# One-core attention and two gated layers: q and k of two runs kept whole, run 0 loaded by head pairs, x in two tiles

## The chip, the cores and the metric

The kernel runs on one core of a Trainium2 chip. The metric is the device time in microseconds (us); lower is better. A profiled execution also leaves a trace, and the trace counts from the first to the last instruction, which it calls the span.

## What is computed

The reference is sliding-window attention with a distance bias, then two gated layers on its output:

```python
scores = scale * np.matmul(q, k.transpose(0, 1, 3, 2))        # 4 batches, 8 heads, 576 positions, 64 wide
mask = (rel >= 0) & (rel < 128)
scores = np.where(mask, scores + bias[None], -1000000000.0)
attn = softmax(scores)                                        # over the keys, float32
x = np.matmul(attn, v)                                        # to 2304 tokens x 512
x = ((x @ w_a) * (x @ w_b)) @ w_out                           # 512 -> 1536 -> 512, weights float64
out = (((x @ w1) * (x @ w2)) @ w3) @ w_out2                   # 512 -> 1024 -> 1024 -> 512
```

q, k, v and the output are float32; the weights come as float64. A product of full precision is made of three TensorE terms of the type fp32r: each operand is split into a rounded `hi` and a rest `lo`, and lo*hi, hi*lo and hi*hi are summed.

## The kernel before

**Attention.** A batch has five blocks of 128 positions (the last has 64), handled in three runs: `RUNS = ((0, 1), (2, 3), (4,))`. A run has four steps, one for each pair of heads, so there are 48 steps in all; steps 0 to 3 are run 0 of batch 0, steps 4 to 7 are run 1, steps 8 to 11 are run 2. A step is: `scores` (TensorE, line 318), `step_exps` (VectorE adds the bias and takes the largest, lines 343 to 348; ScalarE exponentiates, L351), `norms` (VectorE divides by the sum, lines 358 to 365), `probs` (TensorE transposes, L383, then a copy to `pt`), `pv` (TensorE, L404, three steps later: `LAG = 3`) and `pv_out` (ScalarE writes `x_hi`, VectorE writes `x_lo`, lines 418 and 419).

**q and k.** `load_item` brings 128 positions of all heads (256 KB) by one DMA of the SP queue. `prep` transposes them (L282) into PSUM; ScalarE rounds them to `q_th` or `k_th` (L291) and VectorE subtracts the rest into `q_tl` or `k_tl` (L292; the profile shows every such subtraction at line 73, where the helper `sub` is). `scores` then sums the three terms.

**Weights.** `Stages` loads a weight (512 KB), and converts it from float64 in stages: ScalarE makes `ca` (L108) and `ce` (L111), VectorE runs L115, L118, L122 and L127, ScalarE rounds to `wh` (L136), VectorE subtracts to `wl` (line 73). Group 0 has six such weights; two stages' turns are taken in each step of batch 0. A load waits for one of `raws=2` buffers.

**The filler.** Once the six weights of group 0 are whole, `Filler` puts pieces of the first gated layer (`g1`, L546, and `g2_some`, L574) between the steps. The first piece stands behind `pv` of step 4.

**What sets the order.** In the attention part TensorE's order is the program's (`manual_schedule`). The orders of VectorE, ScalarE, GpSimd and SP come from a scheduler that works at build time; each engine then runs its list strictly in order.

**Warm-ups.** `keep_warm` runs matmuls on a constant tile. Ten of 256 columns stand at the start, and `pv` adds one of 512 columns for each full block in batch 0:

```python
            if b == 0 and rn < WARM_RUNS and m == P:
                keep_warm(WARM, warm)
```

**Memory.** `x_hi` and `x_lo` hold all 2304 tokens from the start. The pools `conv_a` and `early_p` (six loads) are closed when group 0's weights are whole, and `acc0` and `acc1` take their place.

Of the kernel before, what the change touches and what calls it, by code (L numbers as in the profile page):

```python
# [29 lines left out]

GROUPS = (6, 4)
TA, TN = 256, 512
LEAD, EARLY, RING = 512, 6, 5
CUTS = (0, 1280, 1792, 2304)
RUNS = ((0, 1), (2, 3), (4,))
LAG = 3
# [1 line left out]
FILL = 1.6  # L38
PACE = (2.0, 1.0)
TURN = 400  # L40
WARM_RUNS, WARM = 3, 1


@with_exitstack
def attention_moe_moe(ctx, tc, q, k, v, w_a, w_b, w_o, w_1, w_2, w_3, w_o2, out):
# [16 lines left out]
    ps_g = ctx.enter_context(tc.tile_pool(name="ps_g", bufs=2, space=PSUM))  # L62

    ident = const.tile([P, P], F32, name="ident")
    x_hi = xp.tile([P, KC, NT], F32R, name="x_hi")
    x_lo = xp.tile([P, KC, NT], F32R, name="x_lo")
    w34 = dram.tile([2, DFF2, DM], F32, name="w34")

    def f32(ap):
# [2 lines left out]
    def sub(eng, out, a, b):  # L72
        eng.tensor_tensor(out=out, in0=a, in1=b, op=ALU.subtract)  # L73
# [177 lines left out]

    def load_item(run, n):
        b, (x, i) = blocks_of(run)[0], items(run)[n]
        if len(items(0)) * run + n < EARLY:
            t = early_p.tile([P, H * D], F32, name="early")
# [16 lines left out]
    def prep(run, n):  # L272
        b, (x, i) = blocks_of(run)[0], items(run)[n]
        m = rows(i)
        hold = []

        def trans():
            ps = ps_t.tile([P, W], F32, name="tr")[:, 0:NP * m].rearrange("p (h c) -> p h c", h=NP)
            hold.append(ps)
            t = raws.pop((b, x, i))  # L280
            for hp in range(NP):
                nc.tensor.transpose(ps[:, hp, :], t[0:m, hp * P:(hp + 1) * P], ident[0:m, 0:m])  # L282

        def parted():
            ps = hold[0]
            if x == 0 and m == LAST:
                dst = [(slice(j * D, (j + 1) * D), q_t2, slice(j * D, (j + 1) * D)) for j in range(2)]
            else:
                dst = [(slice(0, P), k_t if x else q_t, slice(i * P, i * P + m))]
            for o, (hi, lo), c in dst:  # L290
                nc.scalar.activation(hi[o, :, c], ps[o], ACTF.Copy)  # L291
                sub(nc.vector, lo[o, :, c], ps[o], f32(hi[o, :, c]))  # L292

        return trans, parted

# [9 lines left out]
    def scores(st):  # L305
        b, rn, hp = st
        run = RUNS[rn]
        wide = [window(i)[3] == 2 for i in run]
        ps = [ps_s.tile([P, W], F32, name="s") for j in range(2 if any(wide) else 1)]
        at = 0  # L310
        for i in run:
            m, n, nb, nj = window(i)
            ks = slice(max(i - 1, 0) * P, max(i - 1, 0) * P + n)
            for x, (a, c) in enumerate(((1, 0), (0, 1), (0, 0))):
                for j in range(nj):
                    r = slice(j * D, (j + 1) * D) if nj == 2 else slice(0, P)
                    qs = q_t[a][r, hp, i * P:(i + 1) * P] if nj == 2 else q_t2[a][:, hp, :]
                    nc.tensor.matmul(  # L318
                        ps[j][:, at:at + n], qs, k_t[c][r, hp, ks], start=(x == 0), stop=(x == 2)
                    )  # L320
            live[st, i] = dict(ps=[p[:, at:at + n] for p in ps[:nj]])
            at += n
        assert at <= W
# [63 lines left out]
    ready = [0]  # L387
    outs = {}

    def pv(step):  # L390


        b, rn, hp = step
        ps = outs[step] = ps_t.tile([P, W], F32, name="tr")
        at = 0
        for i in RUNS[rn]:
            m, n, nb, nj = window(i)
            t = live.pop((step, i))["pt"]
            for g in range(nb):
# [12 lines left out]
    def pv_out(step):  # L412
        b, rn, hp = step
        run = RUNS[rn]
        m = sum(window(i)[0] for i in run)
        o = slice(b * S + run[0] * P, b * S + run[0] * P + m)
        ps = outs.pop(step)[:, :m]
        nc.scalar.activation(x_hi[:, hp, o], ps, ACTF.Copy)
        sub(nc.vector, x_lo[:, hp, o], ps, f32(x_hi[:, hp, o]))
        if hp == NP - 1:  # L420
            ready[0] = o.stop

# [102 lines left out]
    def g1(g, n, t, tn, zs=range(2), ps=None):  # L525
# [11 lines left out]
        for z in zs:  # L537

            if g:
                ps.append(mm_tile(tn))  # L540
            elif ps[z] is None:
                ps[z] = mm_tile(tn)
            p = ps[z]
            terms = [(w, x, kk) for w, x in ((lo, x_hi), (hi, x_lo), (hi, x_hi)) for kk in range(KC)]
            for y, (w, x, kk) in enumerate(terms):
                nc.tensor.matmul(  # L546
                    p, w[:, z, kk, :], x[:, kk, o], start=(y == 0), stop=(y == len(terms) - 1)
                )
        if zs[-1] == 0:
            return  # L550
# [41 lines left out]
    def g2_feat(g, t, m, tn):  # L592
# [8 lines left out]
        ya = acc[h].rearrange("p (m t) -> p m t", m=KC)[:, m, t0:t0 + tn]  # L601
        nc.vector.tensor_tensor(out=ya, in0=ya, in1=p, op=ALU.add)  # L602
        if g == G1 - 1:
            nc.scalar.activation(x_hi[:, m, o], ya, ACTF.Copy)
            sub(nc.gpsimd, x_lo[:, m, o], ya, f32(x_hi[:, m, o]))

    def g2_tok(g, t, s, tn):
        p = mm_tile(DM)
# [66 lines left out]
    def attention_ops():  # L675

        late = []
        for n in range(NS + LAG):
# [24 lines left out]
    class Filler:  # L703
# [5 lines left out]
        def run(self, owed):  # L709
            self.owed += owed  # L710
            while self.owed > 0 and self.items:
# [2 lines left out]
                    break  # L714
                self.items.pop(0)
                self.owed -= cost
                f()
            self.owed = min(self.owed, 1.0)

# [5 lines left out]
    pools["A", 0] = ctx.enter_context(tc.tile_pool(name="wA0", bufs=1))  # L725
    pools["A", 1] = ctx.enter_context(tc.tile_pool(name="wA1", bufs=1))
    first = ExitStack()
    pools.update(conv=first.enter_context(tc.tile_pool(name="conv_a", bufs=1)), raws=2, cas=3)
    early_p = first.enter_context(tc.tile_pool(name="early_p", bufs=EARLY))
    pools["gate"] = gate_pa  # L730
    pools.update(abufs=1, gbufs=2)

    consts()
    for x in range(len(items(0))):
        load_item(0, x)
    for x in range(len(RUNS[0])):
        load_v(0, x)
    for x in range(len(items(1))):
        load_item(1, x)
        f, g = prep(0, x)  # L740
        f()
        g()
    side.parts += weight_parts(0)
    fl = Filler()
    nc.vector.memset(warm, 0.0)
# [66 lines left out]
```

## Time and profile before

| | |
|---|---|
| runs | median 963.18 us (962.84 to 963.54, 3 runs) |
| profiled execution | 965.76 us, its span 964.0 us, mean granted TensorE clock 0.986 |
| TensorE matmul (PE) | 944.0 us busy, 98% |
| weight load (PEld) | 787.4 us, 82% |
| VectorE (DVE) | 552.1 us, 57% |
| ScalarE (ACT) | 420.6 us, 44% |
| GpSimd (POOL) | 156.9 us, 16% |
| chain that ended last | PE 91%, DVE 5%, ACT 2%, DMA 1% |

Busy shares are means over 964 us. The first 50 us differ from the rest, so the rows below are read by stretch. A matmul in float32 leaves two records in the trace, one in fp32r leaves one. "Granted clock" is a share of full speed: 1.00 is 2.4 GHz, 0.50 is 1.2 GHz.

### The profile page before, as it was taken

To read this page: it belongs to the slowest core of one execution; us is meant where nothing else is said; L and a number is where in the kernel's file an instruction comes from. 1 tells how busy PE (TensorE), PEld (TensorE's weight loads), DVE (VectorE), ACT (ScalarE), POOL (GpSimd) and SP (SyncE) were. 2 spreads that over 40 slices of the span, in tenths; PEclk is the share of its full clock that TensorE was granted. 3 is DMA by queue.
4 is the path that set the end of the run, shared out by engine and by line. 5 is a ranking of instruction groups with operands and counts; after the bars stand their busy time and mean duration, and the time that the engine had idled before them with its cause. 6 is when DMAs were issued, how large, how long until landed. Compare 5 with 4: busy or idle time off the path is not lost.

```text
span 964.0 us, 13974 instructions
## 1 busy us (share of the span) xinstructions
PE 944.0 (98%) x5330; PEld 787.4 (82%) x5330; DVE 552.1 (57%) x1312; ACT 420.6 (44%) x939; POOL 156.9 (16%) x139
## 2 busy tenths in 40 slices
PE   7899999999999999999999999999999999999998
PEld 5588788787888888888888888888888888888886
DVE  6968786854998355866745653822832822521322
ACT  5867777855654344444533531533421421211111
POOL 3000010001112110211110121344212111111111
PEclk8799999999999999999999999999999999999999
DMA  9523333002443222332312320300300300000112
GB/s 213 154 57 71 83 77 68 18 2 88 132 137 103 77 88 91 106 99 78 130 46 97 109 88 1 111 21 0 110 22 1 109 22 1 23 1 0 44 56 99
DMA packets 90371, 68.28 MB, mean 71 GB/s; under 512 B 58304, under 2 KB 79296, under 8 KB 90304
## 3 DMA queue, kind: packets, MB, share of 16 engines
q1 hardware_dynamic: 90304, 67.38, 24.1%
q8 instruction: 42, 0.69, 0.3%
q14 instruction: 25, 0.20, 0.1%
HBM read 58.20 MB, written 8.91 MB: 70 GB/s over the span
## 4 chain that ended last, share of the span: by engine, by line
PE 91%; DVE 5%; ACT 2%; DMA 1%; issue 0%; SPq 0%; POOL 0%; DVEq 0%
PE mm L546 51%; PE mm L598 13%; PE mm L613 10%; PE mm L454 5%; PE tr L404 3%; PE s L318 2%; PE tr L383 2%; PE mm L574 2%; PE tr L282 1%; DVE pe L345 1%; DVE pe L365 1%; ACT pe L351 1%; PE mm L446 1%; PE mm L586 1%; DMA early<-in_k 1%
## 5 line engine op out<-in xcount | busy, mean ns | idle before, releaser
L73 POOL TENSOR_TENSOR gl<-g,gh 128x512 fp32r<-128x512 f32 (+1 forms) x102 | 124.4, 1219 | 790.3 <-ACT gh L558 790.3
L555 DVE TENSOR_TENSOR g<-a,mm 128x512 f32<-128x512 f32 (+1 forms) x102 | 63.4, 622 | 203.1 <-PE mm L546 198.3
L558 ACT ACTIVATE gh<-g 128x512 fp32r<-128x512 f32 (+1 forms) x102 | 59.1, 579 | 152.9 <-DVE g L555 152.4
L553 ACT ACTIVATE a<-mm 128x512 f32<-128x512 f32 (+1 forms) x102 | 55.2, 541 | 126.2 <-PE mm L546 126.2
L546 PE MATMUL mm<-x_hi,wlA 128*128 128x512 f32 (+1 forms) x416 | 102.9, 368 | 0.0
L546 PE MATMUL mm<-x_lo,whA 128*128 128x512 f32 (+1 forms) x416 | 99.6, 361 | 0.0
L546 PE MATMUL mm<-x_hi,whA 128*128 128x512 f32 (+1 forms) x416 | 99.4, 361 | 0.0
L546 PE MATMUL mm<-x_hi,wlB 128*128 128x512 f32 (+1 forms) x400 | 98.9, 369 | 0.1
L546 PE MATMUL mm<-x_lo,whB 128*128 128x512 f32 (+1 forms) x400 | 98.6, 368 | 0.0
L546 PE MATMUL mm<-x_hi,whB 128*128 128x512 f32 (+1 forms) x400 | 98.2, 368 | 0.0
L111 ACT ACTIVATE ce<-raw,pad 128x512 int32<-128x512 uint32 x76 | 57.9, 762 | 65.9 <-DVE ca L127 33.8
L546 PEld LDWEIGHTS mm<-x_lo,whA 128*128 128x128 f32 x416 | 72.5, 189 | 12.2
L546 PEld LDWEIGHTS mm<-x_hi,whA 128*128 128x128 f32 x416 | 72.5, 189 | 12.0
L546 PEld LDWEIGHTS mm<-x_hi,wlB 128*128 128x128 f32 x400 | 71.1, 188 | 13.1 <-ACT acc L590 0.5
L546 PEld LDWEIGHTS mm<-x_lo,whB 128*128 128x128 f32 x400 | 71.1, 189 | 12.5
L546 PEld LDWEIGHTS mm<-x_hi,whB 128*128 128x128 f32 x400 | 71.0, 189 | 12.5
L602 DVE TENSOR_TENSOR acc<-acc,mm 128x512 f32<-128x512 f32 (+1 forms) x100 | 62.2, 629 | 33.1 <-PE mm L598 32.9
L546 PEld LDWEIGHTS mm<-x_hi,wlA 128*128 128x128 f32 x416 | 71.3, 189 | 11.6 <-issue 0.3
L108 ACT ACTIVATE ca<-raw 128x512 f32<-128x512 f32 x76 | 50.6, 666 | 51.0 <-DMA raw<-in_moe_w 23.2
L351 ACT ACTIVATE pe<-pe,st 128x256 f32<-128x256 f32 (+1 forms) x144 | 68.4, 478 | 9.7 <-DVE st L345 9.3
L127 DVE SCALAR_TENSOR_TENSOR ca<-ce,ca 128x512 int32<-128x512 int32 x76 | 58.9, 775 | 13.1 <-ACT ce L111 11.6
L122 DVE SCALAR_TENSOR_TENSOR ca<-raw,ca 128x512 int32<-128x512 int32 x76 | 58.8, 775 | 1.7
(121 smaller groups left out, 1579.2 us busy)
## 6 DMA issues: line engine op xcount, KB each, us to landing
raw<-in_moe_w SPq DMA_DIRECT2D x32, 512.0 KB, 3.6
raw<-in_moe_w_out SPq DMA_DIRECT2D x20, 512.0 KB, 3.5
raw<-in_moe_w_a SPq DMA_DIRECT2D x12, 512.0 KB, 3.6
raw<-in_moe_w_b SPq DMA_DIRECT2D x12, 512.0 KB, 3.5
out<-acc SPq DMA_DIRECT2D x18, 256.0 KB, 2.0
v<-in_v SPq DMA_DIRECT2D x16, 256.0 KB, 4.1
w<-ce SPq DMA_DIRECT2D x16, 256.0 KB, 2.0
raw<-w SPq DMA_DIRECT2D x16, 256.0 KB, 2.9
```

What stands on the lines that cost most here:

```text
L73: eng.tensor_tensor(out=out, in0=a, in1=b, op=ALU.subtract)
L111: nc.scalar.activation(e, lw, ACTF.Relu, bias=seven, scale=-(2.0 ** -29))
L122: nc.vector.scalar_tensor_tensor(out=ai, in0=hw, scalar=-(1 << 30), in1=ai, op0=ALU.bitwise_and, op1=ALU.bitwise_or)
L127: nc.vector.scalar_tensor_tensor(out=ai, in0=es[0], scalar=7, in1=ai, op0=ALU.bitwise_xor, op1=ALU.bitwise_or)
L351: nc.scalar.activation(pe[:, j, :n], pe[:, j, :n], ACTF.Exp, bias=st[:, 0, j:j + 1], scale=-1.0, accum_out=st[:, 1, j:j + 1],)
L546: nc.tensor.matmul(p, w[:, z, kk, :], x[:, kk, o], start=(y == 0), stop=(y == len(terms) - 1))
L553: nc.scalar.activation(a, ps[0], ACTF.Copy)
L555: nc.vector.tensor_tensor(out=gg, in0=a, in1=ps[1], op=ALU.mult)
L558: nc.scalar.activation(gh, gg, ACTF.Copy)
L598: nc.tensor.matmul(p, w, x, start=(y == 0), stop=(y == len(terms) - 1))
L602: nc.vector.tensor_tensor(out=ya, in0=ya, in1=p, op=ALU.add)
L613: nc.tensor.matmul(p, x, w, start=(y == 0), stop=(y == len(terms) - 1))
```

## The change

Five edits go together. (1) `x` is two pairs of tiles: tokens 0 to 1279 from the start, the rest only once the first pools are closed. `pv_out` cuts a step that straddles token 1280 in two. (2) For runs 0 and 1, q and k go unsplit to `w_t` (float32), and their scores are one float32 term in place of three; only k of block 3 is also split, because run 2 needs it. (3) Run 0's q and k come by head pairs: sixteen loads of 64 KB, four for each pair, each pair transposed ahead of its step (`prep_first`). (4) Weights have four load buffers in place of two, and all four loads of run 1 have buffers of their own. (5) The warm-ups in `pv` end with the first filler piece.

```diff
-LEAD, EARLY, RING = 512, 6, 5
+LEAD, EARLY, RING = 512, 4, 5
+WHOLE = 2
...
-WARM_RUNS, WARM = 3, 1
...
-    x_hi = xp.tile([P, KC, NT], F32R, name="x_hi")
-    x_lo = xp.tile([P, KC, NT], F32R, name="x_lo")
+    HALF = CUTS[1]
+    x_t = [[xp.tile([P, KC, HALF], F32R, name=f"x_{z}") for z in ("hi", "lo")]]
...
+    def load_first(hp, x):
+        t = raws[x, hp] = early_p.tile([P, 2, P], F32, name=f"first{x}{hp}")
+        for i in range(2):
+            nc.sync.dma_start(
+                out=t[:, i].rearrange("p (h d) -> p h d", h=2),
+                in_=(q, k)[x][0, 2 * hp:2 * hp + 2, i * P:(i + 1) * P, :].rearrange("h p d -> p h d"),
+            )
...
+            if run < WHOLE:
+                nc.scalar.activation(w_t[x][:, :, i * P:(i + 1) * P], ps, ACTF.Copy)
+                if x == 0 or i < blocks_of(WHOLE - 1)[1][-1]:
+                    return
...
+    def prep_first(hp):
...
+            for x in range(2):
+                raw = raws.pop((x, hp))
+                for i in range(2):
+                    nc.tensor.transpose(ps[:, x, i], raw[:, i], ident)
...
+            for x in range(2):
+                ps = hold[0][:, x].rearrange("p i c -> p (i c)")
+                nc.scalar.activation(w_t[x][:, hp, 0:2 * P], ps, ACTF.Copy)
...
-            for x, (a, c) in enumerate(((1, 0), (0, 1), (0, 0))):
+            one = b == 0 and rn < WHOLE
+            terms = ((0, 0),) if one else ((1, 0), (0, 1), (0, 0))
+            for x, (a, c) in enumerate(terms):
+                qh, kh = (w_t[0], w_t[1]) if one else (q_t[a], k_t[c])
...
-            if b == 0 and rn < WARM_RUNS and m == P:
-                keep_warm(WARM, warm)
+            if not began[0] and m == P:
+                keep_warm(1, warm)
...
+        cut = [o.start] + [HALF] * (o.start < HALF < o.stop) + [o.stop]
+        for a, e in zip(cut, cut[1:]):
+            hi, lo = [t[:, hp] for t in xs(slice(a, e))]
...
+            if run == 0 and hp + 1 < NP:
+                ops += prep_first(hp + 1)
...
-    pools.update(conv=first.enter_context(tc.tile_pool(name="conv_a", bufs=1)), raws=2, cas=3)
-    early_p = first.enter_context(tc.tile_pool(name="early_p", bufs=EARLY))
+    pools.update(conv=first.enter_context(tc.tile_pool(name="conv_a", bufs=1)), raws=4, cas=3)
+    whole_p = first.enter_context(tc.tile_pool(name="whole_p", bufs=1))
+    w_t = [whole_p.tile([P, NP, WHOLE * 2 * P], F32, name=f"w_{x}") for x in "qk"]
+    early_p = first.enter_context(tc.tile_pool(name="early_p", bufs=1))
...
-    for x in range(len(items(0))):
-        load_item(0, x)
-    for x in range(len(RUNS[0])):
-        load_v(0, x)
+    for hp in range(NP):
+        for x in range(2):
+            load_first(hp, x)
+        if hp in (1, 2):
+            load_v(0, hp - 1)
...
+            late_x = ctx.enter_context(tc.tile_pool(name="xp1", bufs=1))
+            x_t.append([late_x.tile([P, KC, NT - HALF], F32R, name=f"x1_{z}") for z in ("hi", "lo")])
```

The lines of the changed kernel stand some 5 to 40 further down: its scores are at L356, bias and largest at L383, ScalarE's exponentials at L389, the division at L403, the weight conversion at L113, L116, L120, L123, L127, L132 and L141, `sub` at L78.

TensorE's start, from the first transposes of q and k (`early` and `first` are loads of them, `tr` and `s` are PSUM tiles) to the scores of step 2. Before:

```order
L282 MATMUL tr<-ident,early 128x128 x16
L318 MATMUL s<-k_th,q_tl 128x128 x2
L318 MATMUL s<-k_tl,q_th 128x128 x2
L318 MATMUL s<-k_th,q_th 128x128 x2
L318 MATMUL s<-k_th,q_tl 128x256 x2
L318 MATMUL s<-k_tl,q_th 128x256 x2
L318 MATMUL s<-k_th,q_th 128x256 x2
L282 MATMUL tr<-ident,early 128x128 x4
```

And now (the ten warm-ups, which stood ahead of it all, are the rows left out):

```order
L322 MATMUL tr<-ident,first_148 128x128 x2
...
L322 MATMUL tr<-ident,first_151 128x128 x2
L356 MATMUL s<-w_k,w_q 128x128 x2
L356 MATMUL s<-w_k,w_q 128x256 x2
L322 MATMUL tr<-ident,first_154 128x128 x2
L322 MATMUL tr<-ident,first_157 128x128 x2
L295 MATMUL tr<-ident,early_176 128x128 x4
L356 MATMUL s<-w_k,w_q 128x128 x2
```

Step 0 needs one head pair in place of all four; the transposes of block 2's q (`early_176`) still stand ahead of the scores of step 1.

ScalarE around the first weight conversion (`ca` and `ce` are the converted weight's tiles, `pt` the transposed probabilities). Before:

```order
L351 ACTIVATE pe,st<-pe,st 128x128
L291 ACTIVATE k_th<-tr 128x4x128
L351 ACTIVATE pe,st<-pe,st 128x256
L268 ACTIVATE pt<-tr 128x512
L291 ACTIVATE q_th<-tr 128x4x128
L108 ACTIVATE ca<-raw 128x512
L111 ACTIVATE ce<-raw,pad 128x512
L351 ACTIVATE pe,st<-pe,st 128x128
```

And now, from the copies of head pair 2 (first two rows) to those of head pair 3 (last two):

```order
L327 ACTIVATE w_q<-tr 128x256
L327 ACTIVATE w_k<-tr 128x256
L304 ACTIVATE w_k<-tr 128x4x128
L281 ACTIVATE pt<-tr 128x512
L389 ACTIVATE pe,st<-pe,st 128x128
L113 ACTIVATE ca<-raw 128x512
L116 ACTIVATE ce<-raw,pad 128x512
L389 ACTIVATE pe,st<-pe,st 128x256
L389 ACTIVATE pe,st<-pe,st 128x128
L327 ACTIVATE w_q<-tr 128x256
L327 ACTIVATE w_k<-tr 128x256
```

The conversion of the first weight has moved into step 2's exponentials, ahead of the copies that step 3's scores need.

VectorE between the bias rows of step 4 and those of step 5. Before, all of it but the first four rows:

```order
L73 TENSOR_TENSOR wlA_240<-ca,whA_239 128x512
L73 TENSOR_TENSOR x_lo<-tr,x_hi 128x256
L358 TENSOR_SCALAR st<-st 128x4
L270 COPY pt<-tr 128x256
L73 TENSOR_TENSOR q_lastl<-tr,q_lasth 64x4x64
L359 RECIPROCAL st<-st 128x4
L115 TENSOR_SCALAR ca<-ca 128x512
L365 TENSOR_SCALAR pe<-pe,st 128x256 x4
L118 TENSOR_SCALAR ca<-ca 128x512
```

And now, its last eleven rows; ten more of the kind stand ahead of them:

```order
L127 SCALAR_TENSOR_TENSOR ca<-raw,ca 128x512
L78 TENSOR_TENSOR wlA_239<-ca,whA_238 128x512
L120 TENSOR_SCALAR ca<-ca 128x512
L283 COPY pt<-tr 128x256
L397 RECIPROCAL st<-st 128x4
L78 TENSOR_TENSOR q_lastl<-tr,q_lasth 64x4x64
L132 SCALAR_TENSOR_TENSOR ca<-ce,ca 128x512
L123 TENSOR_SCALAR ca<-ca 128x512
L120 TENSOR_SCALAR ca<-ca 128x512
L403 TENSOR_SCALAR pe<-pe,st 128x256 x4
L127 SCALAR_TENSOR_TENSOR ca<-raw,ca 128x512
```

More conversions of weights stand between two steps of the attention than before. From step 4's bias to step 5's division VectorE's list now has 17 rows of conversions, where it had 11: one more each of L123 and L127, two more each of L132 and of the subtraction to `wl`; it has one subtraction to `x_lo` less, and two short rows (128x4) more.

## Rows read from the trace of the kernel before

**Rows 1.** Windows, core 0: stretch, length, busy of each engine (instructions), granted clock, DMA share, GB/s.

```profile
11.00:30.00 19.00, 16.67 (x110) 11.90 (x110) 16.94 (x70) 14.76 (x46) 0.00 (x0) 0.73 1.18 234
30.00:45.00 15.00, 10.79 (x80) 6.58 (x79) 14.94 (x59) 13.61 (x40) 0.00 (x0) 0.81 0.52 155
45.00:50.00 5.00, 5.00 (x36) 3.59 (x34) 4.64 (x16) 3.85 (x8) 0.00 (x0) 0.54 0.03 10
50.00:81.00 31.00, 31.00 (x291) 27.41 (x288) 19.87 (x75) 19.60 (x60) 2.19 (x3) 1.00 0.24 54
...
130.00:165.00 35.00, 35.00 (x331) 29.29 (x330) 27.67 (x119) 28.65 (x90) 2.01 (x2) 1.00 0.29 65
```

**Rows 2.** Waits of PE, whole span: waited for, us in total, times, longest.

```profile
PE tr L383 <- DVE pe L365: 9.0, 8, 2.2
...
PE mm L574 <- POOL gl L73: 0.4, 1, 0.4
```

**Rows 3.** Chain of waits, 0 to 110 us: start, length, what; the start.

```profile
2.79 5.10 DMA early<-in_k
...
10.98 0.29 DVE pe L345
...
11.32 1.87 ACT pe L351 x8
```

**Rows 4.** The same chain, VectorE's pace.

```profile
23.66 0.60 DVE ca L122
...
24.67 0.60 DVE ca L127
...
32.08 0.60 DVE wlA L73
...
35.19 0.34 DVE ca L118
...
38.76 0.33 DVE x_lo L73
```

**Rows 5.** The same chain, from step 5's probabilities on.

```profile
44.41 1.94 PE tr L383 x8
46.35 1.58 PE s L318 x9
47.93 1.05 PE tr L404 x8
...
50.48 4.31 PE mm L546 x36
54.79 0.87 PE tr L383 x8
...
56.02 0.59 PE tr L404 x8
56.60 0.32 PE mm L373
...
102.60 0.95 PE s L318 x12
```

**Rows 6.** Timeline of PE: the start's warm-ups, and block 2's q.

```profile
2.83 2.31 PE L373 MATMUL mm<-warm 128*128 128x256 f16 x10 [2.83 <-DVE warm L745]
...
11.64 0.72 PE L282 MATMUL tr<-ident,early 128*128 128x128 f32 x4 [0.81 <-DMA early<-in_q]
```

**Rows 7.** The first weight: issue on SP, from issue to landing, first use on ACT.

```profile
13.70 0.61 SPq L83 DMA_DIRECT2D raw<-in_moe_w_a  x1
...
DMA to landing us min/median/max: 4.9/4.9/4.9
...
18.68 0.67 ACT L108 ACTIVATE ca<-raw 128x512 f32<-128x512 f32 x1
```

**Rows 8.** Timeline of DVE: step 4's first bias row, step 5's division.

```profile
29.71 0.41 DVE L345 CUSTOM_DVE_ANT_0 pe<-s,relb 128x256 f32<-128x256 f32 x1
...
43.92 1.14 DVE L365 TENSOR_SCALAR pe<-pe,st 128x256 f32<-128x256 f32 x4
```

More of the change, by code (lines that the diff above doesn't have):

```diff
@@ L64, in attention_moe_moe, with xs @@
     ident = const.tile([P, P], F32, name="ident")
-    x_hi = xp.tile([P, KC, NT], F32R, name="x_hi")
-    x_lo = xp.tile([P, KC, NT], F32R, name="x_lo")
+    HALF = CUTS[1]
+    x_t = [[xp.tile([P, KC, HALF], F32R, name=f"x_{z}") for z in ("hi", "lo")]]
+    def xs(o):
+        n = o.start // HALF
+        assert o.stop <= (HALF, NT)[n]
+        return [t[:, :, o.start - n * HALF:o.stop - n * HALF] for t in x_t[n]]
     w34 = dram.tile([2, DFF2, DM], F32, name="w34")
@@ L253, in load_item @@
         b, (x, i) = blocks_of(run)[0], items(run)[n]
-        if len(items(0)) * run + n < EARLY:
-            t = early_p.tile([P, H * D], F32, name="early")
+        if run == 1 and n < EARLY:
+            t = early_p.tile([P, H * D], F32, name=f"early{n}")
         else:
@@ L292, in parted, with trans @@
                 sub(nc.vector, lo[o, :, c], ps[o], f32(hi[o, :, c]))
+        return trans, parted
+    def prep_first(hp):
+        hold = []
+        def trans():
+            ps = ps_t.tile([P, W], F32, name="tr").rearrange("p (x i c) -> p x i c", x=2, i=2)
+            hold.append(ps)
+            for x in range(2):
+                raw = raws.pop((x, hp))
+                for i in range(2):
+                    nc.tensor.transpose(ps[:, x, i], raw[:, i], ident)
+        def parted():
+            for x in range(2):
+                ps = hold[0][:, x].rearrange("p i c -> p (i c)")
+                nc.scalar.activation(w_t[x][:, hp, 0:2 * P], ps, ACTF.Copy)
         return trans, parted
@@ L313, in scores @@
             ks = slice(max(i - 1, 0) * P, max(i - 1, 0) * P + n)
-            for x, (a, c) in enumerate(((1, 0), (0, 1), (0, 0))):
+            one = b == 0 and rn < WHOLE
+            terms = ((0, 0),) if one else ((1, 0), (0, 1), (0, 0))
+            for x, (a, c) in enumerate(terms):
+                qh, kh = (w_t[0], w_t[1]) if one else (q_t[a], k_t[c])
                 for j in range(nj):
                     r = slice(j * D, (j + 1) * D) if nj == 2 else slice(0, P)
-                    qs = q_t[a][r, hp, i * P:(i + 1) * P] if nj == 2 else q_t2[a][:, hp, :]
+                    qs = qh[r, hp, i * P:(i + 1) * P] if nj == 2 else q_t2[a][:, hp, :]
                     nc.tensor.matmul(
-                        ps[j][:, at:at + n], qs, k_t[c][r, hp, ks], start=(x == 0), stop=(x == 2)
+                        ps[j][:, at:at + n], qs, kh[r, hp, ks], start=(x == 0), stop=(x == len(terms) - 1)
                     )
@@ L385, in probs @@
         evict(nc.scalar if i else nc.vector, t, ps)
-    ready = [0]
+    ready, began = [0], [False]
     outs = {}
@@ L417, in pv_out @@
         ps = outs.pop(step)[:, :m]
-        nc.scalar.activation(x_hi[:, hp, o], ps, ACTF.Copy)
-        sub(nc.vector, x_lo[:, hp, o], ps, f32(x_hi[:, hp, o]))
+        cut = [o.start] + [HALF] * (o.start < HALF < o.stop) + [o.stop]
+        for a, e in zip(cut, cut[1:]):
+            hi, lo = [t[:, hp] for t in xs(slice(a, e))]
+            nc.scalar.activation(hi, ps[:, a - o.start:e - o.start], ACTF.Copy)
+            sub(nc.vector, lo, ps[:, a - o.start:e - o.start], f32(hi))
         if hp == NP - 1:
@@ L543, in g1 @@
             p = ps[z]
+            x_hi, x_lo = xs(o)
             terms = [(w, x, kk) for w, x in ((lo, x_hi), (hi, x_lo), (hi, x_hi)) for kk in range(KC)]
@@ L546, in g1 @@
                 nc.tensor.matmul(
-                    p, w[:, z, kk, :], x[:, kk, o], start=(y == 0), stop=(y == len(terms) - 1)
+                    p, w[:, z, kk, :], x[:, kk], start=(y == 0), stop=(y == len(terms) - 1)
                 )
@@ L603, in g2_feat @@
         if g == G1 - 1:
-            nc.scalar.activation(x_hi[:, m, o], ya, ACTF.Copy)
-            sub(nc.gpsimd, x_lo[:, m, o], ya, f32(x_hi[:, m, o]))
+            hi, lo = [x[:, m] for x in xs(o)]
+            nc.scalar.activation(hi, ya, ACTF.Copy)
+            sub(nc.gpsimd, lo, ya, f32(hi))
     def g2_tok(g, t, s, tn):
@@ L716, in run @@
                 self.owed -= cost
+                began[0] = True
                 f()
@@ L733, in attention_moe_moe @@
     consts()
-    for x in range(len(items(0))):
-        load_item(0, x)
-    for x in range(len(RUNS[0])):
-        load_v(0, x)
+    for hp in range(NP):
[3 more added lines that the diff above has]
+            load_v(0, hp - 1)
     for x in range(len(items(1))):
         load_item(1, x)
-        f, g = prep(0, x)
+    for f in prep_first(0):
         f()
-        g()
     side.parts += weight_parts(0)
```

## The prediction, made before the change was run

> **What bounds the kernel now.** I read the windows first. From 50 to 81 us TensorE is busy for 31.00 of 31.00 us, and so it is from 130 to 165 [rows 1]. In the first 45 us it is not: from 30 to 45 it works 10.79 of 15 us while VectorE works 14.94 [rows 1]. So the start is VectorE's, and the rest is TensorE's. The waits say where they meet: TensorE's longest waits are for the division L365, 9.0 us in eight waits [rows 2]. The chain gives the place: step 5's probabilities begin at 44.41, right after VectorE's division of step 5, which starts at 43.92 [rows 5, 8]. From there TensorE never waits until 81 us: transposes, step 7's scores, `pv` of step 4, and the first filler piece at about 50.2 [rows 5]. So the time is, nearly, the moment at which step 5's probabilities begin, plus the work of TensorE behind it. Whatever the change does has to move that moment or take something out of that work.
>
> **Warm-ups taken out.** `began` is set by the first filler piece, so ten of the sixteen warm-ups in `pv` stay, and six go: two each in `pv` of steps 5, 6 and 7. They stand in the stretch where TensorE is never idle, and one costs 0.32 us of the chain [rows 5]. Gain: 6 x 0.32 = 1.9 us, with nothing to hide it.
>
> **The start, up to step 4's bias.** The times of the changed kernel here are estimates, chained from the rows.
> - Step 0. One head pair of q and k is 256 KB, as the first load of before was; it should be there at about 4. But its q now stands ahead of the ten warm-ups, which take 2.31 us [rows 6], and its k behind them: k is transposed at about 6.1, copied by 7.0, scored by 8.4. VectorE's first bias row stood at 10.98, behind four full loads and four subtractions [rows 3]; it comes 2.6 us earlier.
> - Scores in float32. No row shows one. The nearest is `pv`, also float32 and also two heads side by side: eight records, that is four matmuls of 128 columns, take 1.05 us at the low clock and 0.59 at the high one [rows 5], so 0.26 or 0.15 for each. A step of run 0 has six such units (1.6 us low), one of run 1 eight (2.1 low, 1.2 high), beside 1.58 and 0.95 for the three terms of before [rows 5]. I take `pv`'s price; the lower bound is the price of before, the upper one is the two heads one after the other (third rival).
> - Step 1. Its scores still stand behind the transposes of block 2's q. The same 1.8 MB are loaded up to there, so that load lands when it did: TensorE waited for it until 11.64 [rows 6]. Bias of step 1 at about 13.7.
> - Step 2. ScalarE works strictly in order: exponentials of step 1 (1.87 us [rows 3]), then the copies of head pair 2, then the scores: about 17.9.
> - Step 3. Here a new wait comes in. ScalarE's list now has the first weight's `ca` and `ce` in the middle of step 2's exponentials, reached at about 18.7. That weight was issued at 13.70 and landed 4.9 us later, just as it was used at 18.68 [rows 7]. Now the two `relb` loads are ahead of it too (256 KB, some 1 us), so I put it at 19.5. Behind the waiting row stand three exponentials of step 2 and the copies of head pair 3, and TensorE and VectorE wait for these: bias of step 3 at about 23.5.
> - Step 4. VectorE then has some 6.4 us in its list before step 4's bias: about 30.0. Before, that row stood at 29.71 [rows 8].
>
> So the 2.6 us gained at the front are gone by step 4, and 0.3 more: they went into waits in which VectorE idles, while it has done three conversion rows more and, since its first bias row, three subtractions less than before.
>
> **From step 4's bias to step 5's division.** VectorE was busy for 14.94 of 15 us there [rows 1], so its list is the time. The list now has more in it. One more row L118 (now L123) costs 0.34 us, one more L122 0.60, two more L127 (now L132) 1.20, two more subtractions to `wl` 1.20, and one subtraction to `x_lo` less gives back 0.33 [rows 4]: 3.0 us more; the two short rows I leave at nothing. They are no new work. They stood behind step 5's division before, in the 50 to 81 us stretch, where VectorE works 19.87 of 31 us [rows 1] and TensorE sets the pace. Moved ahead of the division, they cost their whole length; the room they leave is worth nothing.
>
> **From there on.** The seven rows of conversions at 0.34 to 0.60 us that remain are covered as before. TensorE's list up to the filler is the same but for step 7's scores (0.5 us dearer at the low clock by `pv`'s price, or not at all; I take nothing, and keep the 0.5 for the range). A step that straddles token 1280 costs four ScalarE and four VectorE rows, in batch 2, where TensorE is busy for 35.00 of 35.00 us [rows 1]; without that cover about 1.5 us. The later tile of x, `acc0` and `acc1` wait only for rows that are long done. In the later groups a few pieces of the first layer change places with the products of `w3`; the only wait there is 0.4 us in all [rows 2], which is the bound either way.
>
> **Sum.** Step 5's probabilities begin 0.3 + 3.0 = 3.3 us later, at 47.7; the warm-ups give back 1.9: +1.4 us. The profiled execution would go from 965.76 to 967.2. It lies 2.6 above the median of the runs, 963.18, so the runs would have a median of **964.6 us**.
>
> **The rivals.**
> - *The gain at the front is kept.* If the weight has landed when ScalarE asks, and the copies do not hold up the scores, VectorE runs through. Between its first bias row and step 4's lay 18.7 us [rows 3, 8]; three subtractions less (1.8 us) and one row each of L115, L118 and L122 more (1.3 us) make 18.2 [rows 4], so step 4's bias comes at 26.6, 3.1 earlier. That pays for the 3.0 us of conversions, and the warm-ups remain: 961.2. If the 2.06 us also go that VectorE idled between 11 and 30 [rows 1], 959.1. For it: less work, a first bias row that is surely earlier. Against it: the order of ScalarE's list. I give it 959 to 961.3 and a chance of 0.25.
> - *TensorE keeps its clock.* From 45 to 50 us the granted clock is 0.54, so it is mostly at 1.2 GHz, though TensorE is busy throughout; from 30 to 45, at 72% busy, it is 0.81 [rows 1]. The same three pieces take 1.94, 1.58 and 1.05 us there and 0.87, 0.95 and 0.59 later [rows 5]: 2.2 us. Should the float32 scores, which hold TensorE longer, and `pv` of step 3, which now runs later, keep it at 2.4 GHz up to step 5's probabilities, the time is 962.4. Against it: TensorE waits as long for VectorE as before. Chance 0.15. The Trainium skill, "TensorE: Matmul & The Clock Gate", section "What's actually happening", has the slow clock as the default, released by activity; by that rule longer scores speak for this rival. The trace agrees as far as unbroken work from 44 to 81 us goes, over which the clock rises from 0.54 to 1.00.
> - *The two heads' float32 scores run one after the other (slower).* A transpose of 128 columns takes 1.94 / 8 = 0.24 us at the low clock [rows 5]; two records of that for each unit make 0.48, so a step of run 0 would take 2.9 us (+1.3) and one of run 1 3.9 (+1.8). Steps 3 and 4 stand in the chain with that, and step 7 in TensorE's own stretch: up to 4.9 us, 969.5. It decides once run 1's scores take over 3 us. For it: no row shows a float32 matmul on half of the array's rows. Against it: `pv`'s halves do overlap, and the scores' own pairs did so in fp32r. Chance 0.12.
>
> **How the numbers follow.** The forecast has 0.48, and its own range is 963.3 to 966.5: from a weight that lands 1 us sooner, to one that lands 1 us later and scores 0.5 us dearer. A measurement of this kernel can tell about 0.2% (1.9 us) from no change, so same is 961.3 to 965.1. Faster: nearly all of the first rival and a small part of the second, 0.28. Slower: the third rival and a little over a third of the forecast's case, 0.30. Same: 0.42. The range leaves out the lower tail of the first rival and the upper half of the third: 958.5 to 968.5.
>
> **What would show it.** Right: step 0's bias near 8.4, step 4's near 30, a ScalarE wait for the first weight near 19, step 5's probabilities near 47.7, and 50 to 81's stretch 1.9 us shorter with ten warm-ups of 512 columns left. The first rival shows as step 4's bias ahead of 27 with no idle VectorE, the second as a granted clock of 1.00 ahead of the filler, the third as scores over 3 us. Wrong altogether: if TensorE waits at another place behind the filler's start, or if the stretch from the filler to the end changes by anything but the warm-ups.

## The result, and the profile after

The changed kernel takes 971.35 us (969.62 to 972.03, 6 runs), against 963.40 us (962.84 to 965.75, 6 runs) of the kernel before on the same chip: a ratio of 1.0077, 95% interval 1.0063 to 1.009. It is slower, and outside the range of the prediction. Its profiled execution took 972.03 us with a span of 970.2, which is 6.2 us more than the profiled execution before; the medians lie 8.0 apart, because the profiled execution before was 2.4 us above its median and this one 0.7. The rows below come from it.

Windows of the changed kernel, columns as in [rows 1]:

```profile
11.00:30.00 19.00, 12.96 (x79) 9.26 (x80) 11.31 (x52) 12.75 (x41) 0.00 (x0) 0.91 1.21 249
30.00:45.00 15.00, 10.25 (x68) 6.05 (x67) 14.91 (x46) 11.28 (x29) 0.00 (x0) 0.77 0.57 136
45.00:57.00 12.00, 9.21 (x59) 5.09 (x56) 11.28 (x44) 10.11 (x32) 0.00 (x0) 0.86 0.20 45
57.00:81.00 24.00, 24.00 (x235) 22.21 (x232) 12.77 (x47) 14.19 (x41) 2.19 (x3) 1.00 0.28 62
```

From 57 us on TensorE is full again, as it was from 50 on before [rows 1]. Ahead of that it is VectorE that now loses time: from 11 to 30 us it works 11.31 of 19 us, where it worked 16.94. It idles 7.7 us there instead of 2.1. The granted clock of 0.91 in that row is no gain over the 0.73 of before: up to 25 us the windows print 1.00 in this execution, but the same eight records of scores took 1.65 us at 14.79 and 0.93 at 19.38 (rows further down).

Waits of TensorE over the whole span (waited for, us in total, times, longest):

```profile
PE tr L421 <- DVE pe L403: 6.3, 6, 1.5
PE tr L421 <- ACT whA L141: 4.7, 1, 4.7
PE s L356 <- ACT w_k L327: 4.0, 2, 3.2
PE tr L295 <- DMA early<-in_q: 3.8, 1, 3.8
PE tr L322 <- DMA first<-in_q: 2.9, 1, 2.9
PE mm L495 <- DVE w3l L489: 1.2, 1, 1.2
PE s L356 <- DVE st L383: 1.2, 2, 0.9
PE mm L487 <- DVE ca L132: 0.8, 1, 0.8
```

The division stands first, as in [rows 2], and the second row, which the profile puts down to ScalarE's `whA`, is a wait for it too: the transposes that waited there read no `whA`, and they begin at 38.40, 0.41 us after VectorE's division of step 3 (37.99, rows below). Together that makes 11.0 us, where it was 9.0. Below it stand waits for loads of q and for ScalarE's copies of k, which cost the kernel before 0.8 and 0.2 us, and, far behind the attention part, two new ones for the products of `w3`.

Where the loads went. SP's queue, timeline (start, length, issue):

```profile
0.72 0.95 SPq L269 DMA_DIRECT2D first<-in_q  x2
...
9.11 0.98 SPq L269 DMA_DIRECT2D first<-in_k  x2
10.14 0.47 SPq L252 DMA_DIRECT2D early<-in_q  x1
...
17.15 0.62 SPq L88 DMA_DIRECT2D raw<-in_moe_w_a  x1
```

Two 64-KB loads take SP 0.95 to 1.09 us, one 256-KB load at 10.14 takes 0.47. The sixteen small loads and two of v are issued only by 10.1, and the first weight follows at 17.15, not 13.70 [rows 7].

The consequence on TensorE, timeline:

```profile
13.75 1.12 PE L295 MATMUL tr<-ident,early 128*128 128x128 f32 x4 [3.84 <-DMA early<-in_q]
14.79 1.65 PE L356 MATMUL s<-w_k,w_q 64*128 64x128 f32 x8
...
19.38 0.93 PE L356 MATMUL s<-w_k,w_q 64*128 64x128 f32 x8
...
25.22 1.22 PE L356 MATMUL s<-w_k,w_q 64*128 64x128 f32 x8 [3.25 <-ACT w_k L327]
...
38.40 1.51 PE L421 MATMUL tr<-ident,pe 128*128 128x128 f32 x6 [4.74 <-ACT whA L141]
...
51.25 1.03 PE L421 MATMUL tr<-ident,pe 128*128 128x128 f32 x6 [1.32 <-DVE pe L403]
...
57.18 0.82 PE L588 MATMUL mm<-x_hi,wlA 128*128 128x256 f32 x4
```

and on ScalarE, which waits for the first weight in the middle of step 2's exponentials:

```profile
22.45 0.66 ACT L113 ACTIVATE ca<-raw 128x512 f32<-128x512 f32 x1 [1.13 <-DMA raw<-in_moe_w_a]
```

Block 2's q is transposed at 13.75, not 11.64 [rows 6]; the weight is used at 22.45, not 18.68 [rows 7]; the scores of step 3 wait 3.25 us for copies that stand behind it; step 5's probabilities begin at 51.25, not 44.41 [rows 5]. VectorE's rows for step 4's bias, step 3's division and step 5's division:

```profile
33.94 0.41 DVE L383 CUSTOM_DVE_ANT_0 pe<-s,relb 128x256 f32<-128x256 f32 x1
...
37.99 0.99 DVE L403 TENSOR_SCALAR pe<-pe,st 128x128 f32<-128x128 f32 x4
...
50.85 0.87 DVE L403 TENSOR_SCALAR pe<-pe,st 128x256 f32<-128x256 f32 x3
```

The first and the last answer to 29.71 and 43.92 [rows 8]: 4.2 us are lost up to step 4's bias, and 2.7 more up to the division. The chain behind it:

```profile
53.07 2.01 PE s L356 x8
55.08 1.05 PE tr L442 x8
...
57.53 4.31 PE mm L588 x36
```

The filler's first group stands in the chain at 57.53 instead of 50.48 [rows 5], 7.05 us later. The same group of 36 takes 4.31 us in both.

Behind that, ScalarE's evictions into x mark the end of attention (last `x_hi<-tr`) and of the first layer (first and last `x_hi<-acc`). Rows by tile x_hi on ScalarE (count, ns of one, first to last start in us), before:

```profile
L418 ACT ACTIVATE x_hi<-tr x48: 201/363/386, 24.5 to 227.4; 128x256 fp32r<-128x256 f32 x32, 128x64 fp32r<-128x64 f32 x16
L604 ACT ACTIVATE x_hi<-acc x20: 400/628/635, 615.8 to 677.9; 128x512 fp32r<-128x512 f32 x16, 128x256 fp32r<-128x256 f32 x4
```

and after:

```profile
L459 ACT ACTIVATE x_hi<-tr x52: 202/362/384, 29.7 to 231.6; 128x256 fp32r<-128x256 f32 x28, 128x64 fp32r<-128x64 f32 x16, 128x128 fp32r<-128x128 f32 x8
L647 ACT ACTIVATE x_hi<-acc x20: 402/627/634, 622.4 to 684.4; 128x512 fp32r<-128x512 f32 x16, 128x256 fp32r<-128x256 f32 x4
```

So the lag is 7.05 us at the filler, 4.2 at the end of attention (the six warm-ups account for 1.9 of the difference), and 6.6 when the first layer ends: 2.4 us are lost between 232 and 622 us, a stretch that the prediction priced at 0.4 at most. Two losses have to be explained, one ahead of 57 us and one behind 232.

### The profile page after: what moved, and what is told of

Read it like the earlier page. It is cut to its first block, busy times and chain, and to the rows that moved or that the text cites. A ratio compares the mean times of both kernels' runs of the same rounds, so it can differ in the third digit from the quotient of the medians.

```text
span 970.2 us, 13909 instructions
## 1 busy us (share of the span) xinstructions
PE 940.3 (97%) x5292; PEld 782.8 (81%) x5292; DVE 550.6 (57%) x1309; ACT 422.0 (43%) x948; POOL 156.5 (16%) x139
## 4 chain that ended last, share of the span: by engine, by line
PE 89%; DVE 6%; ACT 2%; SPq 2%; DMA 1%; issue 1%; POOL 0%; DVEq 0%; ACTq 0%
PE mm L588 51%; PE mm L640 12%; PE mm L656 10%; PE mm L495 5%; PE tr L442 3%; PE s L356 2%; PE tr L421 2%; PE mm L616 2%; DVE pe L383 2%; PE tr L295 1%; DVE pe L403 1%; ACT pe L389 1%; SPq L269 1%; SPq L252 1%; PE mm L487 1%
## 5 line engine op out<-in xcount | busy, mean ns | idle before, releaser
L78 POOL TENSOR_TENSOR gl<-g,gh 128x512 fp32r<-128x512 f32 (+1 forms) x102 | 124.0, 1216 | 797.2 <-ACT gh L600 797.2
L116 ACT ACTIVATE ce<-raw,pad 128x512 int32<-128x512 uint32 x76 | 57.9, 762 | 58.9 <-DVE ca L132 27.3
L113 ACT ACTIVATE ca<-raw 128x512 f32<-128x512 f32 x76 | 50.9, 669 | 57.7 <-DMA raw<-in_moe_w 29.4
L389 ACT ACTIVATE pe<-pe,st 128x256 f32<-128x256 f32 (+1 forms) x144 | 68.4, 478 | 12.0 <-DVE st L383 11.3
L383 DVE CUSTOM_DVE_ANT_0 pe<-s,relb 128x256 f32<-128x256 f32 (+1 forms) x144 | 49.3, 390 | 27.5 <-PE s L356 27.0
L132 DVE SCALAR_TENSOR_TENSOR ca<-ce,ca 128x512 int32<-128x512 int32 x76 | 57.4, 756 | 10.2 <-ACT ce L116 8.5
```

What stands on the lines that cost most here:

```text
L116: nc.scalar.activation(e, lw, ACTF.Relu, bias=seven, scale=-(2.0 ** -29))
L132: nc.vector.scalar_tensor_tensor(out=ai, in0=es[0], scalar=7, in1=ai, op0=ALU.bitwise_xor, op1=ALU.bitwise_or)
L383: nc.vector.tensor_tensor_reduce(out=pe[:, j, :n], in0=ps[j], in1=bias, scale=-1.0 / float(D) ** 0.5, scalar=3.0e38, op0=ALU.add, op1=ALU.min,
L389: nc.scalar.activation(pe[:, j, :n], pe[:, j, :n], ACTF.Exp, bias=st[:, 0, j:j + 1], scale=-1.0, accum_out=st[:, 1, j:j + 1],)
```

## The experiments

Four theories were put to the test. **Theory 1**: the small loads are at fault, by the time SP takes to issue them. **Theory 2**: VectorE's list is at fault, with more conversions of weights ahead of step 5's division (28 of the 30 rows of group 0 in the changed kernel, 20 before); four load buffers in place of two let the scheduler place them there. For the late loss, **theory 3** blames the cut of the warm-ups, through the order that the scheduler then finds for the late stage, and **theory 4** the second tile of x.

What the runs on the start gave, with times in us. "Busy" and "idle" are VectorE's, from its first bias row to step 5's division (both from its timeline, the busy time from the windows). "Late" is from the last `x_hi<-tr` to the first `x_hi<-acc`. Times in a row come from one execution each; five that share the loads of before place the first bias between 10.29 and 10.98, so smaller gaps are not read. The kernel before, run beside each, has medians of 963.4 to 964.1, so the last column compares best.

| kernel | first bias | busy | idle | step 5's division | rows ahead | late | ratio to before, 95% interval |
|---|---|---|---|---|---|---|---|
| before | 10.98 | 30.81 | 2.13 | 43.92 | 20 | 388.4 | 1 |
| changed | 9.01 | 33.27 | 8.57 | 50.85 | 28 | 390.8 | 1.0063 to 1.009 |
| whole loads | 10.70 | 33.99 | 3.52 | 48.21 | 30 | 391.1 | 1.0028 to 1.0054 |
| two queues | 8.61 | 33.92 | 7.57 | 50.10 | 29 | 390.8 | 1.0056 to 1.0083 |
| two buffers | 9.15 | 28.86 | 7.96 | 45.97 | 22 | 390.9 | 1.002 to 1.0055 |
| whole loads, two buffers | 10.70 | 29.07 | 3.58 | 43.35 | 20 | 390.8 | 0.999 to 1.0009 |
| two queues, two buffers | 9.55 | 29.06 | 6.58 | 45.19 | 22 | 390.7 | 1.0006 to 1.0025 |
| before, small loads | 16.02 | 31.00 | 3.02 | 50.04 | 24 | 388.4 | 1.0073 to 1.01 |

**Run 0's q and k in four loads of 256 KB** (the changed kernel otherwise):

```diff
     def load_first(hp, x):
-        t = raws[x, hp] = early_p.tile([P, 2, P], F32, name=f"first{x}{hp}")
-        for i in range(2):
-            nc.sync.dma_start(...)
+        t = raws[x, hp] = early_p.tile([P, H * D], F32, name=f"first{x}{hp}")
+        load(t, x, 0, hp)
...
```

> The changed kernel, but run 0's q and k come by four loads of 256 KB in place of sixteen of 64 KB; the head pairs are still transposed one at a time. Theory 1 (SP takes about 0.51 us to issue a load of any size, so sixteen small ones hold back block 2's q and the first weight): block 2's q is issued near 6.4 us instead of 10.1 and lands near 11.6, the first weight is issued near 14 instead of 17.15, step 4's bias comes 3 to 4 us earlier than 34.0, and the time falls by 3 to 4 us, to about 967.5. Theory 2 (the list of VectorE, with more conversions ahead of step 5's division, sets the start): step 4's bias moves, but step 5's division stays within 1 us of 50.9, and the time stays above 970.

It took 967.70 us, 3.6 less than the changed kernel. SP's queue:

```profile
6.12 1.14 SPq L252 DMA_DIRECT2D early<-in_q  x1
...
13.40 0.61 SPq L88 DMA_DIRECT2D raw<-in_moe_w_a  x1
```

Block 2's q is issued 4.0 us sooner. The weight is issued 3.75 us sooner, but not by the size of the loads alone: the scheduler also put the two `relb` loads, which take SP 1.7 us in the changed kernel, behind it. The first bias comes 1.7 us later, since a head pair now needs whole loads, but VectorE's idle time falls from 8.57 to 3.52 us. Its busy time does not fall: all 30 conversion rows now stand ahead of step 5's division. So step 4's bias, expected 3 to 4 us sooner, came only 0.8 sooner (33.12), behind 18.96 us of VectorE's work in place of 16.45; the gain shows at the division.

**k's small loads issued by ScalarE's queue** (`(nc.sync, nc.scalar)[x].dma_start(...)` in `load_first`):

> The changed kernel, with the eight small loads of run 0's k issued on ScalarE's queue instead of SP's; sizes and bytes are the same. Theory 1: eight issues of 0.51 us leave SP, block 2's q is issued about 4 us earlier (near 6.2), and the time falls by 3 to 4 us. A rival of it (small loads are slow because of their size, whoever issues them): block 2's q still lands near 13.7, and the time stays above 970. Theory 2: the time stays above 970.

It took 970.82 us, no gain that can be told from the changed kernel, though block 2's q was issued at 7.88 and the weight at 14.79. VectorE's idle time falls by only 1.0 us, its list grows by a row, and TensorE's wait for ScalarE's copies `w_k` grows from 4.0 to 5.1 us. Theory 1 had expected 3 to 4 us. Block 2's q was issued 2.3 us sooner here, against 4.0 with whole loads, and gave 0.5 us against 3.6, so earlier issue does not explain by itself what the whole loads gave. The Trainium skill, "DMA: Bandwidth & Descriptors", section "Issuing engines are not separate DMA queues", says that a second issuing engine saves only the sequencer's time, and that this is usually small against the transfer. The trace agrees on the first part: issue came 2.3 us sooner. On the second it does not for a row of 64-KB loads: the eight pairs at 0.95 to 1.09 us take SP 8.0 us in the changed kernel, while each load lands some 2.5 us after its issue.

**Two buffers for weights** (the changed kernel with `raws=4` set back to `raws=2`):

> The changed kernel with two load buffers for weights, as before, in place of four. Theory 2: VectorE has some five conversion rows fewer ahead of step 5's division, which comes 2 to 3 us earlier than 50.9, and the time falls by 2 to 3 us. Theory 1: the first weight still lands near 22.4 and the start is as late as it was; the time changes by less than 1 us.

It took 966.79 us, 4.6 less. The first weight is issued as late as in the changed kernel (17.09), and VectorE idles 7.96 us; but 22 conversion rows stand ahead of the division in place of 28, and VectorE's work up to there falls by 4.4 us. This is theory 2 by itself, and larger than expected.

**The kernel before with sixteen small loads** into its own tiles:

```diff
+    for hp in range(NP):
+        for x in range(2):
+            for i in range(2):
+                nc.sync.dma_start(
+                    out=raws[0, x, i][:, hp * P:(hp + 1) * P].rearrange("p (h d) -> p h d", h=2),
+                    in_=(q, k)[x][0, 2 * hp:2 * hp + 2, i * P:(i + 1) * P, :].rearrange("h p d -> p h d"))
...
```

> The kernel before, with only run 0's q and k brought by sixteen loads of 64 KB into the same four tiles (and the two loads of v between them). Theory 1: block 2's q is issued about 3.7 us later than 6.41, the first weight about 3.4 us later than 13.70, and the kernel is slower by 2 to 4 us than before. The rival (the loads' order is hidden behind VectorE's work in the kernel before): within 1 us of before.

It took 972.05 us, 7.9 more than before and twice the expected price: this kernel needs all head pairs for step 0, so its first bias waits for the last small load and moves from 10.98 to 16.02. In this kernel the small loads alone cost as much as the whole change does.

**Both cures together**, whole loads and two buffers:

> The changed kernel with both edits: run 0's q and k in four loads of 256 KB, and two load buffers for weights. Alone they gave 3.6 and 4.6 us. Additive: 971.35 - 8.2 = 963.2, with the two waits at w3 still in it and 20 rows of conversions ahead of step 5's division. If they remove the same loss twice, it stays at the better of the two, 966.8.

It took 963.67 us, a ratio of 1.0 (0.999 to 1.0009). The two gains nearly add up: 7.7 us together, 3.6 and 4.6 alone. The table shows why they do. The loads decide how long VectorE idles (8.57 and 7.96 us with small ones, 3.52 and 3.58 with whole ones), the buffers how much it has to do ahead of the division (33.27 and 33.99 us with four, 28.86 and 29.07 with two).

**The same two buffers with the second queue**:

> The changed kernel with k's small loads issued on ScalarE's queue and with two load buffers for weights; 22 rows of conversions ahead of step 5's division. With four buffers the second queue gave 0.5 us, though the first weight was issued 2.4 us earlier. Theory 1 and 2 together: the earlier loads were then spent on more conversions ahead of step 5 (29 rows); with two buffers they are kept, 966.8 - 1.5 to 2 = 965. Rival: small loads cost the same whichever queue issues them, 966.8.

It took 965.31 us, 1.5 better than two buffers alone. The second queue pays now, but VectorE still idles 6.58 us. TensorE waits 4.7 us for `w_k` there, 2.0 with whole loads: ScalarE's list, with the weight's rows ahead of the copies, keeps that part of the loss. How the rest of the small loads' cost divides between SP's issue and that list is open.

**The late stage: only the warm-ups cut.** The kernel before with the change's edit (5) and nothing else:

```diff
-            if b == 0 and rn < WARM_RUNS and m == P:
-                keep_warm(WARM, warm)
+            if not began[0] and m == P:
+                keep_warm(1, warm)
...
```

> The kernel before with one edit of the change alone: the warm-ups in pv end with the first filler piece (six fewer). Theory 3: the 2 us that every version of the changed kernel so far lost behind the attention part, with two new waits of TensorE near the products of w3 (1.2 and 0.8 us), come from this edit: the order of that stage is found at build time, and without the six rows TensorE's list there is another one (a w3 transpose stands alone ahead of its product, where two stood together). Then the time is 964.1 - 1.9 + 2.0 = 964.2, no gain, and the two waits are in the profile. Theory 4: those waits come from the second tile of x, and this edit only removes work: 964.1 - 1.9 = 962.2, and no such wait.

It took 963.73 us beside 963.47 of before, a ratio of 0.9999 (0.9987 to 1.001): no gain. Rows by tile x_hi:

```profile
L418 ACT ACTIVATE x_hi<-tr x48: 200/365/385, 23.8 to 222.1; 128x256 fp32r<-128x256 f32 x32, 128x64 fp32r<-128x64 f32 x16
L604 ACT ACTIVATE x_hi<-acc x20: 402/624/635, 612.7 to 674.9; 128x512 fp32r<-128x512 f32 x16, 128x256 fp32r<-128x256 f32 x4
```

The late stretch is 390.6 us, 2.2 more than before, and TensorE's timeline has both waits:

```profile
332.65 1.03 PE L446 MATMUL mm<-ident,ca 128*128 128x128 f32 x8
...
334.45 0.66 PE L446 MATMUL mm<-ident,ca 128*128 128x128 f32 x4 [0.77 <-DVE ca L127]
335.05 1.20 PE L454 MATMUL mm<-oh,w3l 128*128 128x512 f32 x4
...
501.88 1.20 PE L454 MATMUL mm<-oh,w3l 128*128 128x512 f32 x4 [1.25 <-DVE w3l L448]
```

Transposes of `w3` (L446) stand one behind the other and the product (L454) right after. Before, TensorE had pieces of the first layer between them:

```profile
338.30 0.60 PE L446 MATMUL mm<-ident,ca 128*128 128x128 f32 x4
338.65 1.17 PE L546 MATMUL mm<-x_hi,wlA 128*128 128x512 f32 x4
339.66 1.08 PE L546 MATMUL mm<-x_lo,whA 128*128 128x512 f32 x4
340.58 1.07 PE L546 MATMUL mm<-x_hi,whA 128*128 128x512 f32 x4
341.49 1.07 PE L454 MATMUL mm<-oh,w3l 128*128 128x512 f32 x4
```

Those 2.8 us covered the eviction and subtraction that make `w3h` and `w3l`.

**The kernel before with warm-ups in run 0 alone** (`WARM_RUNS, WARM = 1, 1`, eight fewer):

> The kernel before, with warm-ups in pv of run 0 alone (eight fewer, those of steps 4 to 7). Its list of the late stage is the same as before's. Theory 3: no late waits, 964.1 - 8 x 0.32 = 961.5, or 962.1 if the two of step 4 were hidden behind VectorE. Theory 4 says the same of this run; it tells whether a cut of warm-ups pays at all. A third way: without them TensorE's clock falls and the time is above 964.

It took 961.21 us, a ratio of 0.9971 (0.996 to 0.9982), 2.3 us less than before. Its list in the late stage is that of before, the waits are absent, and the late stretch takes 388.3 us. So cutting warm-ups pays, unless the scheduler answers with another order.

**The changed kernel with all sixteen warm-ups kept**:

> The changed kernel with all sixteen warm-ups in pv kept, as before; x stays in two tiles. Theory 3: 1.9 us more up to 81 us, 2.0 us less behind it, 971.4 in all, and no wait at w3. Theory 4: 971.4 + 1.9 = 973.3, with both waits.

It took 970.49 us (1.0056 to 1.0088 of before), as theory 3 said; theory 4's 973.3 lies outside. No wait for `w3`, 388.3 us late, with x in two tiles.

**The kernel before with x in two tiles** and nothing else:

> The kernel before with x in two tiles, the second laid out with acc, and nothing else. Four more ScalarE and four more VectorE rows where a step straddles token 1280. The bound of the prediction was 1.5 us for them without cover; theory: they are covered, 963.5 to 964.0, with no wait at w3. Rival: a wait on them in batch 2 or on the later tile, 965 or more.

It took 964.59 us, 1.0 to 1.0024 of before: at most 2.3 us, perhaps nothing. The late stretch is 388.6 us and free of both waits. Theory 4 is out; whether the split costs the 1.5 us of the prediction's bound can't be told.

**Three cures together**: whole loads, two buffers, warm-ups in run 0 alone, on the changed kernel:

> The changed kernel with run 0's q and k in four loads of 256 KB, two load buffers for weights, and warm-ups in pv of run 0 alone. Theory 1 (loads) and theory 2 (VectorE's list) together: block 2's q is issued at 6.1 and the first weight at 13.4, and 20 rows of conversions stand ahead of step 5's division, as before (28 in the changed kernel, 30 with whole loads, 22 with two buffers). Then that division comes at about 43.5 and the filler at about 49.5, against 43.9 and 50.1 before; with the eight warm-ups gone and before's list in the late stage that makes 964.1 - 0.6 - 2.2 = 961.3. If only the loads or only the list counts, it comes out like the better of those two runs without their late waits, 964.8 or above. If theory 4 holds, 2 us more: 963.3 with waits at w3.

It took 961.20 us, 0.9967 (0.9956 to 0.9977). The late stretch is 388.4 us. The division of step 5 came at 44.92, later than forecast, but the filler at 48.9:

```profile
39.35 2.14 PE tr L416 x8
41.49 2.01 PE s L351 x8
...
45.92 0.87 PE tr L416 x8
46.80 1.06 PE s L351 x8
47.86 1.02 PE tr L437 x16
48.89 4.51 PE mm L583 x36
```

TensorE's clock rises in this stretch: the transposes cost 2.14 us at 39 and 0.87 at 46, so that less time lies between division and filler than before [rows 5].

**The kernel before with no warm-ups in `pv`** (`WARM_RUNS = 0`):

> The kernel before with no warm-ups in pv at all; the list of the late stage is before's. Eight more rows go than in the version with warm-ups in run 0 alone (961.2), but they stood where TensorE waits for VectorE. If only TensorE's own work counts: 961.2 again. If they kept TensorE's clock up, the granted clock of 11 to 45 us falls below the 0.82 and 0.89 of that version, the stretch up to the filler gets longer, and the time is 962 or above.

It took 959.97 us, 0.9964 (0.9951 to 0.9976). The granted clock was 0.82 from 11 to 30 us and 0.93 from 30 to 45, against 0.82 and 0.89 with the warm-ups of run 0, so in these two executions they did not keep the clock up. The scheduler found another list for VectorE here, with 18 rows of conversions ahead of step 5's division, which came at 40.95; what of the gain is the warm-ups' own is not shown. By their intervals this kernel, the one with three cures and the one with warm-ups in run 0 alone can't be told apart; each of the three beats both kernels that this study began with, the kernel before by 0.3 to 0.4%.

## Why the prediction was wrong, point by point

**The step that failed is step 1's**: "the same 1.8 MB are loaded up to there, so that load lands when it did". Bytes were counted, not issues. Up to block 2's q there are now sixteen loads of q and k where there were four, and the load was issued at 10.14, 4.0 us later than with whole loads (6.12). Step 1's bias stood at 16.59 instead of the forecast 13.7. The weight's landing, forecast for 19.5 with 1 us for two `relb` loads, came at 22.4 for the same reason: it was issued at 17.15. Each later step passed it on: step 2 was forecast for 17.9 and came at 20.50, step 3 for 23.5 and came at 26.77, step 4 for 30.0 and came at 33.94. Of the forecast's 0.3 us up to step 4's bias, 4.2 were measured. The whole loads undo the late issue: step 1's bias comes at 15.28, and they gave back 3.6 us of time; the kernel before with small loads alone lost 7.9. But the loads are not all of the 4.2 us. With two buffers alone step 4's bias comes at 32.20, with whole loads alone at 33.12, and only with both at 30.56, near the forecast 30.0.

**Step 0** was right: its bias was forecast for 8.4 and came at 9.01, 2.0 us ahead of before. It was worth nothing, as the forecast said, because the waits behind it took more.

**ScalarE's wait for the first weight** was right as a mechanism, with its place, and 3 us late in time. The Trainium skill, "PSUM — Partial Sum Buffer", section "Engine vs sequencer instructions", has ScalarE's and VectorE's queues as strictly first in, first out; the row at 22.45, with three exponentials and the copies of head pair 3 behind it, agrees.

**The conversions ahead of step 5's division**, 3.0 us, were right: from step 4's bias to the division 16.91 us passed instead of 14.21, 2.7 more, of which VectorE worked 16.82. (In the trace one of the 17 rows, a subtraction to `wl` at 51.63, falls inside the division and holds its last transposes up by 0.36 us.) But only those behind step 4's bias were priced. Counted from the start there are eight more rows than before, and two buffers in place of four, which remove six of the eight, gave 4.6 us.

**The warm-ups** gave about their 1.9 us, and lost more. From the filler to the last `x_hi<-tr` the kernel before takes 173.4 us with six fewer, and 175.6 with all sixteen and x in two tiles. The forecast let them act on TensorE's attention part alone, and held the late stage's change of order to 0.4 us, the only wait there. It is 2.4 us in the changed kernel and 2.2 with the warm-up edit alone. This was the second failed step, and "if the stretch from the filler to the end changes by anything but the warm-ups" was the sign set for it. Why six warm-ups fewer change that order, and eight or sixteen fewer do not, lies in the build-time scheduler and stays open.

**The sum** by measured terms, for the filler and behind it: 4.2 up to step 4's bias, 2.7 for the list, 0.1 up to the filler make 7.05; less 1.9 for the warm-ups, less 0.9 between filler and the end of attention, plus 2.4 late, less 0.4 that no experiment assigns behind 622 us: 6.2, the difference of the spans.

**The 0.9 us** are no gain of the change. From 90 to 115 us the granted clock of the profiled execution before is 0.93, of the changed kernel and of the kernel before with x in two tiles 1.00; near 195 us the kernel before and the changed kernel have a drop each (0.93 from 185 to 210), the kernel with x in two tiles has none. It takes 175.6 us from filler to the end of attention, where the kernel before, with two drops, took 177.3. This is also part of why the spans lie closer than the medians.

**The range.** The forecast's own range is a little wider than its terms: 964.6 less 1.0, and plus 1.0 and 0.5, gives 963.6 to 966.1, not 963.3 to 966.5; the measured time lies outside both.

**The rivals.** The gain at the front was not kept: VectorE idled 8.57 us up to the division, not less than before. TensorE did not keep its clock: 0.77 from 30 to 45 us and 0.86 up to 57, and `pv` cost 1.05 us just ahead of the filler, as before [rows 5]. The heads' scores do not run one after the other: a step of run 1 takes 2.0 us at the low clock, as forecast by `pv`'s price, not 3.9. The slower side was thus given to the wrong mechanism.

**What was left of the change's idea.** With whole loads and two buffers, whole q and k save VectorE 1.7 us up to step 5's division (29.07 against 30.81), and 1.5 us more idle time takes most of that back. TensorE then waits for ScalarE's copies, 2.0 us in all. With whole loads and two buffers the change is as fast as the kernel before; with warm-ups in run 0 alone as well it takes 961.20 us, where the kernel before with that same cut takes 961.21. Apart from the warm-ups, the change without its faults is worth nothing that can be measured.

## What to carry to other kernels

Count a load's issue as well as its bytes: a queue that issues sixteen small loads pushes back everything behind them, above all a first weight for which an engine waits in order. More buffers let work start earlier; where an engine's list sets the pace, look at what that work is placed in front of. And where a scheduler sets the order, an edit at the front is finished only when the list of the last stage has been compared too: a gain of 1.9 us at 60 us was undone by two waits at 334 and 502 us.

## What had not been expected of the hardware

SP took as long to issue a 64-KB load (0.95 us for two) as a 256-KB one that stood first (0.43 us for the first of the whole loads) or behind small ones (0.47 for block 2's q in the changed kernel). The whole loads behind that first one take 0.56 to 1.32 us each, and yet more data moves: up to 11 us the windows show 138 GB/s with small loads, 182 with whole ones. And two heads' float32 matmuls on half of the array's rows each overlap: with k's loads on ScalarE's queue, a step's eight records of run 0 took 1.65 us at a granted clock of 0.50 (from 22.85) and 0.93 at 1.00 (from 7.53), where the third rival had priced 2.9 at the low clock for one after the other.
